# Chunks 5 to 7 of an MLP input normalised with columns on partitions, beside a long convolution

## The chip, the core and the metric

The kernel runs on one core of a Trainium2 chip. The core has five engines with an instruction stream each: TensorE (PE, matmuls; its weight loads are shown as PEld), VectorE (DVE), ScalarE (ACT), GpSimd (POOL) and SyncE (SP, which here only issues DMAs). DMAs are also issued from ACT's and POOL's streams. Engines wait for one another through semaphores; each works through its own stream in order. SBUF is the on-chip memory with 128 partitions, PSUM is the accumulator memory that PE writes. The metric is the device time of one execution in microseconds, the median of several runs.

## What is computed

```python
xn = _layernorm(x, axis=-1)              # x = A_q, 2048 rows of 448
out = x + _A_ref(xn, k, v, shift_k, ssm_k, ssm_D) + _B_ref(xn, w1, b1, w2)

# A: short causal convolution of k (4 taps), times v, then a causal convolution
#    of length 2048 per column with ssm_k (by FFT), plus kv * ssm_D; gated: xn * y
# B: h = xn @ w1 + b1 (448 -> 1792); act = h * tanh(softplus(h)); act @ w2 (1792 -> 448)
```

## The kernel before

**Two programs in one stream.** The MLP (part B) and the convolution (part A) are interleaved by hand. The 2048 rows are eight *chunks* of 256 rows (two tiles `jj` of 128 rows each), and the 1792 hidden columns are seven *pairs* of two blocks of 128. The list `pairs` has 56 entries (chunk c, pair p), entry i = 7c + p. Time is counted in *slots*, two to an entry: in the even slot 2i `mlp_slot` issues the first matmuls of entry i (`g1_mm`, line 463), in the odd slot 2i + 1 the activation (`mish`, line 479) and the second matmuls of entry i - 2 (`g2_mm`, line 493). The plans `plan` (before the MLP's part of a slot), `plan2` (after it) and `plan3` (inside `mish`, between the activations and the split) hang the convolution's steps on slots. The order of each engine's stream is the order in which this Python code runs.

**Precision.** Matmul operands are split into a high part `h` (a rounded copy in float32r, made by ACT) and a low part `l` (the difference, made by DVE): function `split`, lines 73 to 75. Three products of high and low parts are summed. Hence `XH`/`XL` for the input, `ah`/`al` (tiles `ach`, `acl`) for the activations, `w1h`/`w1l`, `w2h`/`w2l` for the weights.

**The input of a chunk.** PE contracts over partitions, so the first matmul needs the normalised input with its 448 columns on partitions (three blocks of 128; the fourth block is the last 64 columns twice, which carries high and low weights). The rows come with rows on partitions. For the next chunk c + 1, during chunk c: `ln_load` loads the rows `Q` at pair 0; `ln_stats` puts the statistics (two `bn_stats`, two `bn_aggr` on DVE, then eps on DVE and the powers on POOL) on a list `drip`, from which `dv()` draws one after other DVE work, and all that are left at p = 4 (`NP - 3`); `ln_norm` at p = 5 norms on ACT (two activations and the tail copy) into `xn`; `ln_T` (line 451) transposes each of the two row tiles by four PE matmuls with an identity (line 437), and splits the result out of PSUM (ACT line 449, DVE line 447): tile 0 in the odd slot of p = 5 ahead of `mish`, tile 1 in the even slot of p = 6 ahead of `g1_mm`.

**The convolution's middle.** In eight *octaves* o, spread over slots 63 to 90 (chunks 4 to 6): loads of `ah` and `av` from DRAM scratch (line 188, on SP), packed matmuls `h2_mm` and `v2_mm` (line 201), copies out of PSUM on ACT (`h2_out` line 212, `v2_out` line 221), six products and sums on DVE (`prod`, line 237), the inverse matmuls `i1_mm` (line 248), copies on ACT (`i1_copy`, line 256) and stores to the scratch `E` on SP (`i1_out`, line 263). `inside` puts `h2_out` and `i1_copy` into `plan3` when their slot is the odd slot of p = 5, else into `plan2`. The matmuls of a step use both PSUM buffers `pc`, so the copies of one step have to be under way before the next step's matmuls.

**The convolution's end.** From slot 94 on, four loads `e_load` from `E` (line 292, the first four on SP), a `fold` for each chunk on DVE (lines 297 and 299), the last inverse matmuls `i2_mm` (line 315; those of chunks 6 and 7 in slot 98, before the first matmul of chunk 7), and the gate on DVE and ACT. `t3` opens the last part of SBUF at its first call and then loads the constant `i2` on SP (line 275).

**The end.** The last entry (chunk 7, p = 6) does its second matmuls for each of the two row tiles, and `g2_evac` adds them to the rows `Q` that already hold input and gated convolution (line 516), and stores them. For the very last tile the addition is in two halves of 224 columns, whose stores are issued from SP (line 519) and ACT (line 520).

Of the kernel before, what the change touches and what calls it, by code (L numbers as in the profile page):

```python
# [7 lines left out]
F32 = mybir.dt.float32  # L8
F32R = mybir.dt.float32r
AF = mybir.ActivationFunctionType  # L10
ALU = mybir.AluOpType
# [3 lines left out]
S, D, F = 2048, 448, 1792  # L15
NJ = 16
NF = F // 128
NP = NF // 2
CH = 256
NCHUNK = S // CH  # L20
# [8 lines left out]
I2_AT = {98: (6, 7), 102: (0, 1), 106: (2, 3), 109: (4, 5)}  # L29
LATE = 2  # L30
MOVED = 3
WARM = (448,) * 3 + (128,)
FILL = ((64,), (128, 128))


@with_exitstack
def tile_kernel(ctx: ExitStack, tc, q, k, v, sk, hT, sD, w1, b1, w2, c_f1, c_g, c_gi, c_i2, out):
    nc = tc.nc
    V = nc.vector

    def pool(name, bufs=1, stack=ctx, **kw):
        return stack.enter_context(tc.tile_pool(name=name, bufs=bufs, **kw))

    cp = pool("consts")
    wp = pool("weights")
    mp = pool("mlp")
# [3 lines left out]
    dp = pool("scratch", space=DRAM)  # L50
# [4 lines left out]
    Dkv = dp.tile([NO * 16, 32, D], F32, name="Dkv")  # L55
    E = dp.tile([2, 2, 32, 2, NCHUNK, 2, D], F32, name="E")

    f1id = cp.tile([128, 2, 128], F32, name="f1id")
    f1, ident = f1id[:, 0], f1id[:, 1]
    mhalf = cp.tile([128, 2], F32, name="mhalf")  # L60
    b1t = cp.tile([128, NF], F32, name="b1t")
    mv = cp.tile([128, NJ, 2], F32, name="mv")
    rstd = cp.tile([128, NJ], F32, name="rstd")
    mone = cp.tile([128, 2], F32, name="mone")
    shift = cp.tile([128, NJ], F32, name="shift")


# [2 lines left out]
    w2h = wp.tile([128, NF, D], F32R, name="w2h")  # L70
    w2l = wp.tile([128, NF, D], F32R, name="w2l")

    def split(h, l, raw):
        nc.scalar.copy(h, raw)  # L74
        V.tensor_sub(l, raw, h)  # L75

    def pc():
        return pcp.tile([128, 2, 512], F32, name="pc")
# [4 lines left out]
    def dv(n=1):  # L83
        for _ in range(n):
            if drip:
                drip.pop(0)()
# [8 lines left out]
        plan2.setdefault(int(slot), []).append((fn, args))  # L95

    def inside(slot, fn, *args):
        (plan3 if slot % 2 and slot // 2 % NP == NP - 2 else plan2).setdefault(int(slot), []).append((fn, args))


    ph1 = ExitStack()
    sp1 = pool("ph1", stack=ph1)
    skb = sp1.tile([128, 4, D], F32, name="skb")
    HT, KR, VT, KV, PS, ST, SD = {}, {}, {}, {}, {}, {}, []

# [162 lines left out]
    EE, QA, Q = {}, {}, {}  # L268
# [10 lines left out]
    def late(c):  # L279
        return c >= NCHUNK - LATE  # L280
# [105 lines left out]
    def ln_parts(c):  # L386
        st = mp.tile([128, 2, 6], F32, name="bst", bufs=2)
        ve = mp.tile([128, 2], F32, name="ve", bufs=2)
        xn = mp.tile([128, 2, D + 64], F32, name="xn", tag="xn", bufs=1)
        XN[c] = xn  # L390

        def stats(jj):
            V.bn_stats(st[:, jj], Q[c][:, jj])

        def aggr(jj):
            V.bn_aggr(mv[:, 2 * c + jj], st[:, jj])  # L396

        def eps(a, b):
            V.tensor_scalar(ve[:, a:b], mv[:, 2 * c + a:2 * c + b, 1], EPS, None, op0=ALU.add)

        def power(a, b):
            r, m = (t[:, 2 * c + a:2 * c + b] for t in (rstd, shift))
            if c:
                nc.gpsimd.tensor_tensor(m, mv[:, 2 * c + a:2 * c + b, 0], mone[:, a:b], op=ALU.mult)  # L404
            nc.gpsimd.tensor_tensor(r, ve[:, a:b], mhalf[:, a:b], op=ALU.pow)
            if c:
                nc.gpsimd.tensor_tensor(m, m, r, op=ALU.mult)

        def norm(jj):
            j = 2 * c + jj  # L410
            if c:
                nc.scalar.activation(xn[:, jj, :D], Q[c][:, jj], AF.Identity, bias=shift[:, j:j + 1],
                                     scale=rstd[:, j:j + 1])
            else:
                V.tensor_scalar(xn[:, jj, :D], Q[c][:, jj], mv[:, j, 0:1], rstd[:, j:j + 1],
                                op0=ALU.subtract, op1=ALU.mult)

        def tail(a, b):
            (nc.scalar.copy if c else V.tensor_copy)(xn[:, a:b, D:], xn[:, a:b, D - 64:D])

        return stats, aggr, eps, power, norm, tail

    def ln_stats(c):
        stats, aggr, eps, power, norm, tail = ln_parts(c)
        drip.extend([lambda: stats(0), lambda: stats(1), lambda: aggr(0), lambda: aggr(1),
                     lambda: [eps(0, 2), power(0, 2)]])
        NORM[c] = norm, tail

    def ln_norm(c):
        norm, tail = NORM.pop(c)  # L430
        norm(0)
        norm(1)
        tail(0, 2)

    def transposes(c, jj, p, k0=0, k1=4):
        for kt in range(k0, k1):
# [2 lines left out]
    def x_tiles(c):  # L439
        XS[c] = (mp.tile([128, 4, CH], F32R, name="XH", tag="XH", bufs=2),  # L440
                 mp.tile([128, 4, CH], F32R, name="XL", tag="XL", bufs=2))
# [9 lines left out]
    def ln_T(c, jj):  # L451
        if jj == 0:
            x_tiles(c)
        p = g1p.tile([128, 2, CH], F32, name="pg1").rearrange("p a b -> p (a b)")
        transposes(c, jj, p)
        for lo in range(2):
            x_split(c, jj, p, lo)
# [21 lines left out]
    def mish(i, s):  # L479
        p = pairs[i][1]  # L480
        ps = P1.pop(i)
        a = mp.tile([128, 2, CH], F32, name="a", bufs=2)
        for n in range(2):
            nc.scalar.activation(a[:, n], ps[:, n], AF.Mish, bias=b1t[:, 2 * p + n:2 * p + n + 1])  # L484
        for fn, args in plan3.pop(s, ()):
            fn(*args)
        ah = mp.tile([128, 2, CH], F32R, name="ach", bufs=3)
        al = mp.tile([128, 2, CH], F32R, name="acl", bufs=3)
        split(ah, al, a)
        dv()  # L490
        AHL[i] = ah, al

    def g2_mm(i, jjs=(0, 1)):
        c, p = pairs[i]
        ah, al = AHL[i]
        for n in range(2):
            f = 2 * p + n
            for jj in jjs:
                if f == 0:
                    P2[c, jj] = g2p.tile([128, 512], F32, name="pg2")  # L500
                ps = P2[c, jj][:, :D]
                cs = slice(128 * jj, 128 * jj + 128)
                nc.tensor.matmul(ps, ah[:, n, cs], w2h[:, f], start=f == 0, stop=False)  # L503
                nc.tensor.matmul(ps, ah[:, n, cs], w2l[:, f], start=False, stop=False)  # L504
                nc.tensor.matmul(ps, al[:, n, cs], w2h[:, f], start=False, stop=f == NF - 1)  # L505

    def g2_evac(c, jjs=(0, 1)):
        x = Q[c]
        for jj in jjs:
            last = (c, jj) == (NCHUNK - 1, 1)  # L510
            if moved(c):
                nc.scalar.copy(x[:, jj], P2.pop((c, jj))[:, :D])
            else:
                p = P2.pop((c, jj))
                for cs in ((slice(0, D // 2), slice(D // 2, D)) if last else (slice(0, D),)):
                    V.tensor_add(x[:, jj, cs], p[:, cs], x[:, jj, cs])  # L516
                    dv()
            if late(c) and last:
                nc.sync.dma_start(out[:, 2 * c + jj, :D // 2], x[:, jj, :D // 2])
                nc.scalar.dma_start(out[:, 2 * c + jj, D // 2:], x[:, jj, D // 2:])  # L520
            elif late(c):
                nc.sync.dma_start(out[:, 2 * c + jj], x[:, jj])
        if not late(c):
            nc.sync.dma_start(out[:, 2 * c:2 * c + 2], x)

    def mlp_slot(s):
        i, half = divmod(s, 2)
        n = len(pairs)
        j = i - G2_LAG
        if half == 0:  # L530
            if i < n:
                c, p = pairs[i]
                if c + 1 < NCHUNK:
                    if p == (0 if c else 1):
                        ln_load(c + 1)
                    if p == (2 if c else 3):
                        ln_stats(c + 1)
                    if c == 0 or p == NP - 3:
                        dv(len(drip))
                    if p == NP - 2:  # L540
                        ln_norm(c + 1)
                    if p == NP - 1:
                        ln_T(c + 1, 1)
                g1_mm(i)
        else:
            if i < n:
                c, p = pairs[i]
                if p == NP - 2 and c + 1 < NCHUNK:
                    ln_T(c + 1, 0)
                mish(i, s)  # L550
            if 0 <= j < n - 1:
                g2_mm(j)
            elif j == n - 1:
                for jj in range(2):
                    g2_mm(j, (jj,))
                    g2_evac(pairs[j][0], (jj,))


    ctx.enter_context(tc.manual_schedule())
# [69 lines left out]

    V.memset(mhalf, -0.5)  # L630
    V.memset(mone, -1.0)
    one = cp.tile([128, NJ], F32, name="one")
    V.memset(one, 1.0)
    ve0 = cp.tile([128, 2], F32, name="ve0")
    warm = pc()

# [115 lines left out]
```

## Time and profile before

| | us |
|---|---|
| median of 3 runs | 367.59 (367.14 to 368.11) |
| the profiled execution | 368.03 |
| its span in the profile | 366.3 |

The page of the profile gives the busy time of each engine; a busy PE is not PE at its peak, since matmuls are pipelined. The chain of work that ended last is followed back from the last instruction, at each step to what released it or to the instruction before it on its engine. In lists of the chain a line has start, length and what; in lists of the timeline start, length, engine, line, operation, output and input, count, and in brackets the idle time before it with its releaser. Groups of instructions end with busy time, mean duration in ns, and the idle time of the engine ahead of them. SPq, ACTq and POOLq are DMA issues on those engines' streams. All times are from the span's start.

TensorE is granted its full clock in all 40 slices of the span:

```profile
PEclk9999999999999999999999999999999999999999
```

### The profile page before, as it was taken

Reading aid. Unit: us, or ns where it says so; the run is one execution under the profiler, and the core shown is the slowest. Engines: PE = TensorE matmul, PEld = TensorE weight load, DVE = VectorE, ACT = ScalarE, POOL = GpSimd, SP = SyncE. Lnnn points to the kernel's source line nnn. Section 1 sums busy time; section 2 is a strip of 40 time slices with the busy share of each in tenths; the row PEclk is TensorE's granted clock in tenths of the full one; section 3 lists DMA queues with packets and bytes.
Section 4 is the critical chain, followed back from the end, with each engine's and each line's share of the span. In section 5 each row is a group of like instructions: output and inputs, shape, how many; then the busy total and the mean of one; then the engine's idle time right before and its main releaser. Section 6 shows DMA issues by size and latency. Waiting matters only on the chain.

```text
span 366.3 us, 7485 instructions
## 1 busy us (share of the span) xinstructions
PE 360.1 (98%) x3134; PEld 293.2 (80%) x3134; DVE 261.6 (71%) x350; ACT 180.8 (49%) x307; POOL 24.2 (7%) x41
## 2 busy tenths in 40 slices
PE   7999999999999999999999999999999999999995
PEld 2988888888888988988877666666666889889885
DVE  4898748999999997997434747555384833897741
ACT  3987553533525343533355656557565536235450
POOL 2010000300030002000010000010000010112110
PEclk9999999999999999999999999999999999999999
DMA  8799998958499409714776497787483339649964
GB/s 292 270 314 339 370 335 219 252 170 272 100 306 275 122 18 300 201 41 100 264 236 212 142 333 221 273 242 231 177 292 131 150 106 381 226 172 283 226 120 102
DMA packets 32962, 80.73 MB, mean 220 GB/s; under 512 B 2977, under 2 KB 18338, under 8 KB 32930
## 3 DMA queue, kind: packets, MB, share of 16 engines
q1 hardware_dynamic: 25986, 57.08, 44.7%
q10 hardware_dynamic: 5072, 15.39, 15.1%
q0 software_dynamic: 1872, 7.80, 9.7%
q8 instruction: 24, 0.39, 0.5%
q14 instruction: 8, 0.07, 0.1%
HBM read 51.82 MB, written 29.82 MB: 223 GB/s over the span
## 4 chain that ended last, share of the span: by engine, by line
PE 97%; DMA 1%; ACT 0%; DVE 0%; issue 0%; DVEq 0%
PE pg L476 40%; PE pg L503 13%; PE pg L505 12%; PE pg L504 12%; PE pc L201 7%; PE pc L128 4%; PE pc L248 4%; PE pg L437 2%; PE pc L315 2%; DMA x<-in_hT_dram 1%; PE pg L639 0%; ACT L644 0%; DVE qt L516 0%; DVEq L747 0%
## 5 line engine op out<-in xcount | busy, mean ns | idle before, releaser
L484 ACT ACTIVATE a<-pg,b1t 128x256 f32<-128x256 f32 x112 | 47.1, 472 | 97.5 <-PE pg L476 79.6
L476 PE MATMUL pg<-XH,w1h 128*128 128x256 f32 x448 | 91.0, 285 | 0.2
L503 PE MATMUL pg<-w2h,ach 128*128 128x448 f32 x224 | 83.4, 372 | 0.0
L476 PEld LDWEIGHTS pg<-XH,w1h 128*128 128x128 f32 x448 | 69.7, 188 | 16.6 <-issue 13.6
L505 PE MATMUL pg<-w2h,acl 128*128 128x448 f32 x224 | 81.3, 363 | 0.0
L504 PE MATMUL pg<-w2l,ach 128*128 128x448 f32 x224 | 81.2, 362 | 0.0
L75 DVE TENSOR_TENSOR acl<-a,ach 128x512 fp32r<-128x512 f32 x56 | 38.5, 687 | 55.2 <-ACT ach L74 55.2
L476 PE MATMUL pg<-XL,w1h 128*128 128x256 f32 x448 | 69.7, 277 | 0.0
L476 PEld LDWEIGHTS pg<-XL,w1h 128*128 128x128 f32 x448 | 59.5, 188 | 0.0
L476 PE MATMUL pg<-XH,w1l 128*128 128x256 f32 x336 | 56.9, 278 | 0.0
L503 PEld LDWEIGHTS pg<-w2h,ach 128*128 128x128 f32 x224 | 42.0, 187 | 13.7 <-issue 10.1
L476 PEld LDWEIGHTS pg<-XH,w1l 128*128 128x128 f32 x336 | 47.0, 188 | 0.0
L505 PEld LDWEIGHTS pg<-w2h,acl 128*128 128x128 f32 x224 | 42.1, 188 | 2.7
L504 PEld LDWEIGHTS pg<-w2l,ach 128*128 128x128 f32 x224 | 42.1, 188 | 2.3
L74 ACT CAST ach<-a 128x512 fp32r<-128x512 f32 x56 | 34.8, 622 | 1.7
L165 DVE TENSOR_TENSOR x<-x 128x896 f32<-128x896 f32 x24 | 26.2, 1091 | 0.7
L449 ACT CAST XH<-pg 128x512 fp32r<-128x512 f32 (+1 forms) x17 | 9.5, 563 | 25.8 <-PE pg L437 25.7
L447 DVE TENSOR_TENSOR XL<-pg,XH 128x512 fp32r<-128x512 f32 (+1 forms) x17 | 10.9, 653 | 14.9 <-ACT XH L449 14.9
L134 ACT COPY st<-pc 128x896 f32<-128x896 f32 x16 | 14.5, 907 | 14.3 <-PE pc L128 6.0
L135 DVE TENSOR_TENSOR st<-pc,st 128x896 f32<-128x896 f32 x16 | 17.4, 1087 | 5.3 <-ACT st L134 5.0
L404 POOL TENSOR_TENSOR shift<-mv,mone 128x2 f32<-128x2 f32 x7 | 2.0, 287 | 276.5 <-DVE mv L396 276.5
L256 ACT COPY qe<-pc 128x896 f32<-128x896 f32 x16 | 13.8, 914 | 11.8 <-PE pc L248 11.6
(69 smaller groups left out, 390.6 us busy)
## 6 DMA issues: line engine op xcount, KB each, us to landing
Dh<-st ACTq DMA_DIRECT2D x16, 448.0 KB, 5.6
ah<-Dh SPq DMA_DIRECT2D x8, 896.0 KB, 6.3
av<-Dkv SPq DMA_DIRECT2D x8, 896.0 KB, 5.5
E<-qe SPq DMA_DIRECT2D x16, 448.0 KB, 3.7
Dkv<-st ACTq DMA_DIRECT2D x14, 448.0 KB, 6.0
kr<-in_k_dram SPq DMA_DIRECT2D x10, 448.0 KB, 7.6
x<-in_v_dram SPq DMA_DIRECT2D x8, 448.0 KB, 6.1
e<-E SPq DMA_DIRECT2D x4, 896.0 KB, 8.2
```

The costliest lines, as they stand in the source:

```text
L74: nc.scalar.copy(h, raw)
L75: V.tensor_sub(l, raw, h)
L128: nc.tensor.matmul(ps[h][64 * jj:64 * jj + 64, b, :D], f1[rg:rg + 32, 0:64], x[rg:rg + 32, jj], start=True, stop=True, tile_position=(rg, ...
L135: V.tensor_add(st[:, 0], e, st[:, 1])
L165: V.tensor_add(KV[g], KV[g], o)
L201: nc.tensor.matmul(p[32 * t:32 * t + 32, r, :D], g[rs, t, c], a[rs, t], start=True, stop=True, tile_position=(64 * r, 32 * t))
L248: nc.tensor.matmul(ps[t // 2][64 * r:64 * r + 64, t % 2, :D], gi[ts, r, c], Y[o][c][ts, r], start=c == 0, stop=c == 1, tile_position=(32 * ...
L476: nc.tensor.matmul(ps[:, n], l, r, start=n_ == 0, stop=n_ == len(mm) - 1)
L484: nc.scalar.activation(a[:, n], ps[:, n], AF.Mish, bias=b1t[:, 2 * p + n:2 * p + n + 1])
L503: nc.tensor.matmul(ps, ah[:, n, cs], w2h[:, f], start=f == 0, stop=False)
L504: nc.tensor.matmul(ps, ah[:, n, cs], w2l[:, f], start=False, stop=False)
L505: nc.tensor.matmul(ps, al[:, n, cs], w2h[:, f], start=False, stop=f == NF - 1)
```

## The change

For chunks 5, 6 and 7 (`TURNED`) the rows are brought a second time, already turned: the host lays out `qx`, in which the columns stand on partitions (four blocks, the fourth the doubled last 64) and the 256 rows of a chunk along the free dimension. `x_load` loads it on SP into the buffer that `xn` had: for chunk 5 in slot 64 (p = 4 of chunk 4), for the others at p = 2 of the chunk before.

The rows' means and scales are still computed with rows on partitions. They are put side by side into `t4` (128 x 32, four columns used), DVE transposes its 32 x 32 blocks (`ms_store`), four small DMAs store the rows to the DRAM scratch `MS`, and one DMA (`ms_load`) loads means and scales back, the same 2 x 256 numbers to every partition. `x_norm` subtracts and multiplies on DVE over 128 x 1024, and `x_cast` splits the result in one go. There are no transposes, no norm on ACT and no tail for these chunks. For chunks 5 and 6 the small DMAs are on POOL's stream, store and load behind `mish` at p = 3, and the norm at p = 5; for chunk 7 they are on SP's, the store ahead of `mish` at p = 3, load and norm behind `mish` at p = 4. The rest of `drip` is drawn at p = 3 instead of 4. The split stands in the even slot of p = 6 in all three.

`h2_out` and `i1_copy` of slots 67 and 81 (the odd slots of p = 5 in chunks 4 and 5) move out of `mish`, behind it. The tile `f1id` moves from the constants to the first phase's memory. For the very last row tile, the sum over the first twelve blocks is added to `Q` while the last pair's matmuls run, and those of the last pair are done in two ranges of columns, 256 and 192, each followed by its addition and store (`g2_end`).

```diff
+TURNED = (5, 6, 7)
...
     def inside(slot, fn, *args):
-        (plan3 if slot % 2 and slot // 2 % NP == NP - 2 else plan2).setdefault(int(slot), []).append((fn, args))
+        c, p = divmod(slot // 2, NP)
+        (plan3 if slot % 2 and p == NP - 2 and not turned(c + 1) else plan2).setdefault(int(slot), []).append((fn, args))
...
-            if c:
+            if c and not turned(c):
                 nc.gpsimd.tensor_tensor(m, m, r, op=ALU.mult)
+            if turned(c):
+                nc.gpsimd.tensor_tensor(t4[:, a:b], mv[:, 2 * c + a:2 * c + b, 0], one[:, a:b], op=ALU.mult)
+                nc.gpsimd.tensor_tensor(t4[:, 2 + a:2 + b], ve[:, a:b], mhalf[:, a:b], op=ALU.pow)
...
+    def x_load(c):
+        XN[c] = mp.tile([128, 4, CH], F32, name="xt", tag="xn", bufs=1)
+        nc.sync.dma_start(XN[c], qx[:, TURNED.index(c)])
...
+    def ms_store(c):
+        t, eng = (t3, nc.sync) if c == NCHUNK - 1 else (t2, nc.gpsimd)
+        tT = t([128, 32], "tT", 1)
+        V.transpose(tT, t4)
+        for b in range(4):
+            eng.dma_start(MS[c, :, :, b].rearrange("i j r -> (i j) r"), tT[32 * b:32 * b + 4])
+
+    def ms_load(c):
+        t, eng = (t3, nc.sync) if c == NCHUNK - 1 else (t2, nc.gpsimd)
+        BC[c] = t([128, 2, CH], "bc", 1)
+        eng.dma_start(BC[c], MS[c].rearrange("i j b r -> i (j b r)").partition_broadcast(128))
+
+    def x_norm(c):
+        for i, op in enumerate((V.tensor_sub, V.tensor_mul)):
+            op(XN[c], XN[c], BC[c][:, i:i + 1].to_broadcast([128, 4, CH]))
+
+    def x_cast(c):
+        x_tiles(c)
+        split(*XS[c], XN[c])
...
+    CUT = 256
+
+    def g2_end(i):
+        ah, al = AHL[i]
+        x = Q[NCHUNK - 1][:, 1]
+        for cols, eng in ((slice(0, CUT), nc.sync), (slice(CUT, D), nc.scalar)):
+            ps = pc()[:, 0, :cols.stop - cols.start]
+            for n in range(2):
+                f = NF - 2 + n
+                for k, (l, r) in enumerate(((ah, w2h), (ah, w2l), (al, w2h))):
+                    nc.tensor.matmul(ps, l[:, n, 128:256], r[:, f, cols], start=n + k == 0, stop=n + k == 3)
+            V.tensor_add(x[:, cols], ps, x[:, cols])
+            eng.dma_start(out[:, NJ - 1, cols], x[:, cols])
...
-                    if c == 0 or p == NP - 3:
+                    if c == 0 or p == (NP - 4 if turned(c + 1) else NP - 3):
                         dv(len(drip))
-                    if p == NP - 2:
+                    if turned(c + 1):
+                        if p == (4 if c + 1 == TURNED[0] else 2):
+                            x_load(c + 1)
+                        if p == NP - 1:
+                            x_cast(c + 1)
+                    elif p == NP - 2:
                         ln_norm(c + 1)
-                    if p == NP - 1:
+                    elif p == NP - 1:
                         ln_T(c + 1, 1)
...
-                if p == NP - 2 and c + 1 < NCHUNK:
+                t = turned(c + 1) and c + 1 < NCHUNK
+                if p == NP - 2 and c + 1 < NCHUNK and not turned(c + 1):
                     ln_T(c + 1, 0)
+                end = c + 1 == NCHUNK - 1
+                if t and p == NP - 4 and end:
+                    ms_store(c + 1)
                 mish(i, s)
+                if t and p == NP - 4 and not end:
+                    ms_store(c + 1)
+                    ms_load(c + 1)
+                if t and p == NP - 3 and end:
+                    ms_load(c + 1)
+                if t and p == (NP - 3 if end else NP - 2):
+                    x_norm(c + 1)
...
             elif j == n - 1:
-                for jj in range(2):
-                    g2_mm(j, (jj,))
-                    g2_evac(pairs[j][0], (jj,))
+                x = Q[NCHUNK - 1][:, 1]
+                V.tensor_add(x, P2.pop((NCHUNK - 1, 1))[:, :D], x)
+                g2_mm(j, (0,))
+                g2_evac(pairs[j][0], (0,))
+                g2_end(j)
```

More of the change, by code (lines that the diff above doesn't have):

```diff
@@ L36, in tile_kernel @@
 @with_exitstack
-def tile_kernel(ctx: ExitStack, tc, q, k, v, sk, hT, sD, w1, b1, w2, c_f1, c_g, c_gi, c_i2, out):
+def tile_kernel(ctx: ExitStack, tc, q, qx, k, v, sk, hT, sD, w1, b1, w2, c_f1, c_g, c_gi, c_i2, out):
     nc = tc.nc
@@ L56, in tile_kernel @@
     E = dp.tile([2, 2, 32, 2, NCHUNK, 2, D], F32, name="E")
-    f1id = cp.tile([128, 2, 128], F32, name="f1id")
-    f1, ident = f1id[:, 0], f1id[:, 1]
+    MS = dp.tile([NCHUNK, 2, 2, 4, 32], F32, name="MS")
+    t4 = cp.tile([128, 32], F32, name="t4")
     mhalf = cp.tile([128, 2], F32, name="mhalf")
@@ L64, in tile_kernel @@
     mone = cp.tile([128, 2], F32, name="mone")
+    one = cp.tile([128, NJ], F32, name="one")
     shift = cp.tile([128, NJ], F32, name="shift")
@@ L75, in split, with turned @@
         V.tensor_sub(l, raw, h)
+    def turned(c):
+        return c in TURNED
     def pc():
@@ L97, in inside @@
     def inside(slot, fn, *args):
-        (plan3 if slot % 2 and slot // 2 % NP == NP - 2 else plan2).setdefault(int(slot), []).append((fn, args))
+        c, p = divmod(slot // 2, NP)
+        (plan3 if slot % 2 and p == NP - 2 and not turned(c + 1) else plan2).setdefault(int(slot), []).append((fn, args))
     ph1 = ExitStack()
     sp1 = pool("ph1", stack=ph1)
+    f1id = sp1.tile([128, 2, 128], F32, name="f1id")
+    f1, ident = f1id[:, 0], f1id[:, 1]
     skb = sp1.tile([128, 4, D], F32, name="skb")
@@ L388, in ln_parts @@
         ve = mp.tile([128, 2], F32, name="ve", bufs=2)
-        xn = mp.tile([128, 2, D + 64], F32, name="xn", tag="xn", bufs=1)
-        XN[c] = xn
+        if not turned(c):
+            XN[c] = xn = mp.tile([128, 2, D + 64], F32, name="xn", tag="xn", bufs=1)
         def stats(jj):
@@ L402, in power @@
             r, m = (t[:, 2 * c + a:2 * c + b] for t in (rstd, shift))
-            if c:
+            if c and not turned(c):
                 nc.gpsimd.tensor_tensor(m, mv[:, 2 * c + a:2 * c + b, 0], mone[:, a:b], op=ALU.mult)
             nc.gpsimd.tensor_tensor(r, ve[:, a:b], mhalf[:, a:b], op=ALU.pow)
-            if c:
+            if c and not turned(c):
                 nc.gpsimd.tensor_tensor(m, m, r, op=ALU.mult)
+            if turned(c):
+                nc.gpsimd.tensor_tensor(t4[:, a:b], mv[:, 2 * c + a:2 * c + b, 0], one[:, a:b], op=ALU.mult)
+                nc.gpsimd.tensor_tensor(t4[:, 2 + a:2 + b], ve[:, a:b], mhalf[:, a:b], op=ALU.pow)
         def norm(jj):
@@ L433, in ln_norm @@
         tail(0, 2)
+    BC = {}
+    def ms_store(c):
[14 more added lines that the diff above has]
+        split(*XS[c], XN[c])
     def transposes(c, jj, p, k0=0, k1=4):
@@ L504, in g2_mm @@
                 nc.tensor.matmul(ps, ah[:, n, cs], w2l[:, f], start=False, stop=False)
-                nc.tensor.matmul(ps, al[:, n, cs], w2h[:, f], start=False, stop=f == NF - 1)
+                nc.tensor.matmul(ps, al[:, n, cs], w2h[:, f], start=False,
+                                 stop=f == (NF - 3 if (c, jj) == (NCHUNK - 1, 1) else NF - 1))
+    CUT = 256
[10 more added lines that the diff above has]
+            eng.dma_start(out[:, NJ - 1, cols], x[:, cols])
     def g2_evac(c, jjs=(0, 1)):
@@ L509, in g2_evac @@
         for jj in jjs:
-            last = (c, jj) == (NCHUNK - 1, 1)
             if moved(c):
@@ L513, in g2_evac @@
             else:
[L514 to L521, printed above, removed]
+                V.tensor_add(x[:, jj], P2.pop((c, jj))[:, :D], x[:, jj])
+                dv()
+            if late(c):
                 nc.sync.dma_start(out[:, 2 * c + jj], x[:, jj])
@@ L631, in tile_kernel @@
     V.memset(mone, -1.0)
-    one = cp.tile([128, NJ], F32, name="one")
     V.memset(one, 1.0)
+    V.memset(t4, 0.0)
     ve0 = cp.tile([128, 2], F32, name="ve0")
@@ L734 @@
     kpad = np.pad(a["A_k"][0], ((4, 0), (0, 0)))
+    qx = lay(a["A_q"][0])[:, :, np.r_[0:D, D - 64:D]].reshape(128, NCHUNK, 2, 4, 128)[:, list(TURNED)]
     arrs = dict(
-        q=lay(a["A_q"][0]), k=np.concatenate([lay(kpad[:S])[:, :, :][:, :4], lay(a["A_k"][0])], axis=1),
+        q=lay(a["A_q"][0]), qx=qx.transpose(4, 1, 3, 2, 0).reshape(128, len(TURNED), 4, CH), k=np.concatenate([lay(kpad[:S])[:, :, :][:, :4], lay(a["A_k"][0])], axis=1),
         v=lay(a["A_v"][0]), sk=a["A_shift_k"].T, hT=lay(a["A_ssm_k"].T), sD=a["A_ssm_D"][None],
```

## The prediction

> **What bounds the kernel now.** I read the page first, then the chain of work that ended last in order of time, then the groups by form, the timeline around the places that the diff touches, and the DMA issues.
>
> ```profile
> span 366.3 us, 7485 instructions
> PE 360.1 (98%) x3134; PEld 293.2 (80%) x3134; DVE 261.6 (71%) x350; ACT 180.8 (49%) x307; POOL 24.2 (7%) x41
> PE 97%; DMA 1%; ACT 0%; DVE 0%; issue 0%; DVEq 0%
> ```
>
> The third line is the chain: 97% of the span is TensorE following itself. So a microsecond of matmul taken out of the PE stream is a microsecond of time, unless another engine is then late; and added DVE, ACT or DMA work is free as long as no PE instruction waits for it. The profiled execution took 368.03 us, its span 366.3, the rest lies around it; the median of the runs is 367.59, so I subtract 0.44 at the end.
>
> **The transposes.** The pieces of the chain (start, length, what) around the transposes (L437) of chunks 5, 6 and 7, with neighbours that have none:
>
> ```profile
> 197.31 0.58 PE pg L437 x4
> 197.89 0.21 PE pg L503
> ...
> 201.97 0.59 PE pg L437 x4
> 202.56 2.59 PE pg L476 x22
> ...
> 211.12 2.71 PE pg L476 x22
> ...
> 215.49 0.40 PE pg L503
> ...
> 258.82 0.59 PE pg L437 x4
> 259.41 0.20 PE pg L503
> ...
> 263.48 0.59 PE pg L437 x4
> 264.07 2.51 PE pg L476 x22
> ...
> 304.81 2.51 PE pg L476 x22
> 307.32 0.44 PE pg L437 x4
> ...
> 310.17 0.44 PE pg L437 x4
> 310.61 2.59 PE pg L476 x22
> 313.20 0.21 PE pg L503
> ...
> 315.61 1.66 PE pc L315 x32
> ...
> 362.15 0.21 PE pg L505
> ```
>
> A group of four costs 0.44 between two full-width groups and 0.58 to 0.59 after the packed convolution matmuls. But the first matmul after the packed ones pays that step in any case: L503 is 0.40 there (215.49) and 0.21 behind a transpose, L476 is 2.71 there (211.12) and 2.51 to 2.59 behind one. So taking the transposes out gives: chunk 5, 0.58 + 0.21 - 0.40 = 0.39 and 0.59 + 2.59 - 2.71 = 0.47, together 0.86; chunk 6, 0.59 + 0.20 - 0.40 = 0.39 and 0.59 + 2.51 - 2.71 = 0.39, together 0.78; chunk 7, 0.44 + 0.21 - 0.21 = 0.44 and 0.44 + 2.59 - 2.51 = 0.52, together 0.96. **Sum 2.60 us.** Check: 24 transposes at 0.44/4 = 0.11 are 2.64.
>
> **What takes their place.**
>
> ```profile
> L75 DVE TENSOR_TENSOR acl<-a,ach 128x512 fp32r<-128x512 f32 x56 | 38.5, 687 | 55.2 <-ACT ach L74 55.2
> L165 DVE TENSOR_TENSOR x<-x 128x896 f32<-128x896 f32 x24 | 26.2, 1091 | 0.7
> L516 DVE TENSOR_TENSOR qt<-pg,qt 128x448 f32<-128x448 f32 x9 | 5.2, 616 | 3.8 <-PE pg L505 3.8
> L516 DVE TENSOR_TENSOR qt<-pg,qt 128x224 f32<-128x224 f32 x2 | 0.7, 386 | 0.6 <-PE pg L505 0.6
> L355 ACT CAST w1h<-kr 128x1024 fp32r<-128x1024 f32 x6 | 6.3, 1049 | 0.5 <-DMA kr<-in_w_dram 0.3
> L405 POOL TENSOR_TENSOR rstd<-ve,mhalf 128x2 f32<-128x2 f32 x7 | 6.9, 986 | 3.9 <-DVE ve L399 3.3
> L292 POOL DMA_DIRECT2D e<-E x4 | 3.0, 755 | 25.9 <-PE pc L315 25.8
> ```
>
> Per chunk DVE gets two operations of 128x1024: from 512 wide at 0.69 and 896 at 1.09 the slope is 1.05 ns a column, so 1.23 us each, 2.45 together; one 1.23 us subtract replaces two of 512. ACT loses the norm, its tail and two casts, and gets one cast of 1.05. POOL gets one more pow, about 1 us. Nothing of this is on PE, and it is free if the next PE reader still finds its data:
>
> ```profile
> 269.14 1.08 DVE L237 TENSOR_TENSOR yc<-yc,yd 128x896 f32<-128x896 f32 x1
> ...
> 270.79 1.01 PE L248 MATMUL pc<-ya,gi 32*64 32x448 f32 x16
> ...
> 296.57 1.85 SPq L263 DMA_DIRECT2D E<-qe  x2
> 298.48 0.60 SPq L275 DMA_DIRECT2D i<-in_c_i_dram  x1
> ...
> 309.81 0.69 DVE L75 TENSOR_TENSOR acl<-a,ach 128x512 fp32r<-128x512 f32 x1 [0.70 <-ACT ach L74]
> 310.42 1.09 DVE L297 TENSOR_TENSOR ex<-e 128x896 f32<-128x896 f32 x1
> ...
> 312.55 1.08 DVE L297 TENSOR_TENSOR ex<-e 128x896 f32<-128x896 f32 x1
> ...
> 363.11 0.36 ACTq L520 DMA_DIRECT2D out_dram<-qt  x1
> ```
>
> *Chunks 5 and 6, among the octaves.* The tightest place is chunk 6: the last product ends at 270.22 and PE wants it at 270.79, 0.57 us of slack. Before, DVE stood there behind casts that ACT made after the transposes. After, the last activation pair of chunk 5 no longer waits for them: I follow DVE through the split, 2.45 of norm, four products, the 1.23 subtract and two products, and it ends near 268.3 where PE, 1.64 earlier, comes at 269.2: slack 0.9, no stall. In chunk 5 the same walk leaves 1.7. The turned means have two pairs of some 8.6 us (202.56 to 211.12): four stores and a load at 0.76 us each on POOL's queue, and two landings of at most 4.3 (below), are 12.4 of 17. The h2 and inverse copies that move out of the mish (slots 67 and 81) come behind one 0.62 cast and gain the wait for the transposes. Cost: 0. If this cover were gone, each microsecond of late products would be one of PE.
>
> *Chunk 7, on SP.* Here is the new wait.
>
> ```profile
> e<-E SPq DMA_DIRECT2D x4, 896.0 KB, 8.2
> E<-qe SPq DMA_DIRECT2D x16, 448.0 KB, 3.7
> g<-in_c_g_dram SPq DMA_DIRECT2D x8, 128.0 KB, 4.3
> skb<-in_sk_dram SPq DMA_DIRECT2D x1, 896.0 KB, 9.9
> out_dram<-qt SPq DMA_DIRECT2D x1, 112.0 KB, 1.7
> ```
>
> (size, median us to landing.) SP ends the E stores at 298.42 and the i2 load at 299.08; PE's lead of 1.64 makes that 297.44. By then t4 is there, since the statistics are drawn one pair sooner. Four stores at 0.36 to 0.60 of issue, 1.7 to 3.7 to land, the load's issue, and 1.7 to 4.3 to land: the broadcast arrives between 302.7 and 308.4; I take 304.6, nearest the small rows, as nothing else is in the queues then. Behind the norm on DVE stand, in order, a split (0.61 of pitch), two folds (2.13 each, from 310.42 to 312.55) and the second half of the split of chunk 7's input. PE wants the second fold half way through L315, 316.44 - 2.60 = 313.84. So the limit for the arrival is 313.84 - 2.45 - 0.61 - 4.26 = **306.5**; two microseconds to spare, and up to 1.9 of stall at the slow end. On SP itself the four e loads are held behind the broadcast load, issued near 302.2 instead of 299.5: the second lands within 8.2, near 310.9, and its fold may start at 311.7. Also held, narrowly.
>
> The Trainium skill ("DMA: Bandwidth & Descriptors", Anatomy of one DMA) gives a DMA a fixed cost of about 2.0 us; by it the arrival would be an estimated 304. The 1.7 us row agrees roughly, the 3.7 and 4.3 rows are of larger transfers.
>
> The three copies of q are 512 KB each on SP, behind av's load, so they delay no load that PE is near to; cost 0 to a few tenths, taken as 0.
>
> **The end.** PE's last twelve matmuls of 448 take 0.20 each (362.15). After: six of 448, 1.20; six of 256 at 2.51/22 = 0.114, 0.68; six of 192, which no row has: between 0.114 x 192/256 = 0.086 and 0.114, so 0.52 to 0.68, I take 0.60. PE ends 0.08 later (0 to 0.16). Behind it before: two adds, then the last issue at 363.11, 0.75 after PE's end at 362.36. After: one add of 192, 386 - 32 x 1.03 = 353 ns, and the issue, 0.41 after. The add of the partial sum lies beside twelve matmuls' time. **Gain 0.34 - 0.08 = 0.26**, 0.18 to 0.34.
>
> A rule speaks against narrow matmuls: the Trainium skill ("TensorE: Matmul & The Clock Gate", LDWEIGHTS) has a weight load take columns/1.2 ns, 107 ns for 128 columns, which would keep six matmuls of 192 at 0.64 and the gain at 0.22. No row here is narrow enough to settle it.
>
> **Sum.** 2.60 + 0.26 = 2.86; 368.03 - 2.86 = 365.17, less 0.44: **364.7 us**.
>
> **Rivals.**
> - *Chunk 7's statistics come late* (arrival past 306.5): a stall at L315 of 0 to 1.9, so 364.7 to 366.6. For it: two DMA round trips in series on one in-order queue. Against: an idle chip's DMA. 0.20.
> - *The narrow end costs more*: if 192 and 256 columns ran at the packed f32 pace (1.66/32 x 8 = 0.415 for 448), 192 would take 0.18, PE ends 0.48 + 0.08 later: 365.2. 0.08.
> - *Nothing gained*: PE's place is taken by ACT or DVE in the octaves, where each pair has three evacuations; the 2.6 us become waits and the time stays at 367.3 to 367.6. Against: chain 97% PE and ACT 49% busy. 0.12.
> - *Slower*: the broadcast of one row to 128 partitions is slow by its form. The one such row, skb, took 9.9 us. With that landing the arrival is 302 + 0.4 + 9.9 = 312.3, the stall 5.8, the time 370.5. It decides against the change from an arrival of 306.5 + 2.9 = 309.4 on. Against: skb moved 3.5 times the bytes while all weights were loading. 0.08.
> - My forecast: 0.52.
>
> **Numbers.** About 0.3% (1.1 us) is what a measurement of this kernel can tell from no change. Faster: forecast, late statistics and narrow end, 0.80; within: 0.12; slower: 0.08. The range is 363.9 (a few short waits of PE on ACT go too) to 366.6 (the slow end of the late statistics); it leaves out the last two rivals.
>
> **What would show it.** No L437 in chunks 5 to 7 and PE's chain still near 97%; PE's start of chunk 7's first L476 2.6 earlier; SP's broadcast load landing before 306.5 and DVE's folds without a wait ahead of them; the last matmuls at 0.09 to 0.11 and the last issue 0.4 after PE's end. Wrong would be a PE wait on DVE at L315 or L248, or an idle DVE ahead of the new norm that ends on a DMA and is followed by an idle PE.

## The result and the profile after

The changed kernel takes 364.95 us in the median of 8 runs (364.41 to 367.31), the kernel before 367.62 beside it (8 runs, 366.77 to 368.78). The ratio is 0.9939 with a 95% interval of 0.9918 to 0.9960. 364.7 was forecast. Two of the six runs of experiment 5, at 401.59 and 848.23 us, fell in a slow state and are left out of its figures.

| | before | after |
|---|---|---|
| profiled execution, us | 368.03 | 364.76 |
| its span | 366.3 | 363.0 |

The head of the page of the changed kernel and its chain by engine:

```profile
span 363.0 us, 7477 instructions
PE 357.9 (99%) x3116; PEld 291.1 (80%) x3116; DVE 269.5 (74%) x358; ACT 175.8 (48%) x295; POOL 31.7 (9%) x51
...
PE 99%; DVE 0%; issue 0%
```

DVE got 8 us more work and ACT lost 5, and the chain is still PE following itself. To place the gain, two marks of the chain of the kernel before: the last forward transform of the convolution, which ends before anything is turned, and the last octave's inverse matmuls.

```profile
173.43 0.94 PE pc L128 x16
...
293.10 1.69 PE pc L248 x32
```

The same marks in the chain of the changed kernel (L137, L257), with the places where transposes stood, the last inverse matmuls (L324) and the end:

```profile
172.65 0.94 PE pc L137 x16
...
200.80 2.71 PE pg L514 x22
...
261.46 2.72 PE pg L514 x22
...
290.70 1.69 PE pc L257 x32
...
307.31 2.51 PE pg L514 x22
312.23 1.67 PE pc L324 x32
...
357.77 1.36 PE pc L556 x12
359.16 0.36 DVE qt L557
```

Between the marks lie 119.67 us before and 118.05 after: chunks 5 and 6 gave **1.62**. From the second mark to L324 (315.61 before) it is 22.51 and 21.53: chunk 7 gave **0.98**. The experiments below repeat both numbers: with all three chunks turned the two stretches were 118.05 to 118.15 and 21.52 or 21.53 in six more profiles (`x1`, `x3`, `x5`, `x9`, `x10`, `x11`); with nothing turned (`x8`) they were 119.75 and 22.51. No transposes (L437 before, L475 in the changed kernel) are left there, and the first wide matmuls behind the packed ones cost 2.71 and 2.72, as they did wherever no transpose took the step for them. The rest of the 3.3 us between the two profiles is not the change's: 0.78 was there ahead of the first mark, and 0.73 of it is there at the first transform, which waited for the very first load and began at 6.82 before, and began at 6.09 after.

### The profile page after: what moved, and what is told of

Read it like the earlier page. It is cut to its first block, busy times and chain, and to the rows that moved or that the text cites. A ratio compares the mean times of both kernels' runs of the same rounds, so it can differ in the third digit from the quotient of the medians.

```text
span 363.0 us, 7477 instructions
## 1 busy us (share of the span) xinstructions
PE 357.9 (99%) x3116; PEld 291.1 (80%) x3116; DVE 269.5 (74%) x358; ACT 175.8 (48%) x295; POOL 31.7 (9%) x51
## 4 chain that ended last, share of the span: by engine, by line
PE 99%; DVE 0%; issue 0%
PE pg L514 40%; PE pg L541 13%; PE pg L543 12%; PE pg L542 12%; PE pc L210 7%; PE pc L137 4%; PE pc L257 4%; PE pc L324 2%; PE pc L704 1%; PE pg L475 1%; PE pc L556 0%; PE pg L704 0%; DVE qt L557 0%; DVE mhalf L695 0%; DVE t L698 0%
## 5 line engine op out<-in xcount | busy, mean ns | idle before, releaser
L414 POOL TENSOR_TENSOR rstd<-ve,mhalf 128x2 f32<-128x2 f32 (+1 forms) x9 | 9.0, 1000 | 132.4 <-DVE ve L408 132.2
L144 DVE TENSOR_TENSOR st<-pc,st 128x896 f32<-128x896 f32 x16 | 17.4, 1086 | 4.2 <-ACT st L143 3.9
L165 DVE TENSOR_TENSOR x<-kr,skb 128x896 f32<-128x896 f32 x16 | 17.3, 1084 | 2.0 <-DMA kr<-in_k_dram 2.0
L145 DVE TENSOR_TENSOR st<-pc,st 128x896 f32<-128x896 f32 x16 | 17.5, 1092 | 0.6
```

The costliest lines, as they stand in the source:

```text
L144: V.tensor_add(st[:, 0], e, st[:, 1])
L145: V.tensor_sub(st[:, 1], e, st[:, 1])
L165: V.tensor_mul(o, KR[g - u // 2], skb[:, u:u + 1].to_broadcast([128, 2, D]))
```

## The experiments

All but one (7) change a single thing in the changed kernel, with what belongs to it; the code is shown in part, and `...` marks what is left out. The theory was: the transposes taken out of PE's stream are the gain; the means' round trips are hidden, chunk 7's with little to spare.

**1. The old end put back** (`x1_old_end`): the last entry's code, `g2_evac` with it, is that of the kernel before.

```diff
...
-                g2_mm(j, (0,))
-                g2_evac(pairs[j][0], (0,))
-                g2_end(j)
+                for jj in range(2):
+                    g2_mm(j, (jj,))
+                    g2_evac(pairs[j][0], (jj,))
```

> The change with the old end: the last row tile is added in two halves of 224 after undivided matmuls. Theory (the transposes out of the PE stream are nearly all of the gain): 2.6 us under the kernel before, 365.0 to 365.2; from the start of the last six matmuls to the last issue 2.12 us again, as before, against 1.94 in the changed kernel. Rival (the end by columns is a large part): 1 us or more of the gain gone, 366 or above.

Measured 364.70 (6 runs, 364.20 to 365.30), beside a kernel before of 367.89: ratio 0.9910 (0.9891 to 0.9928). Nothing of the gain is lost without the new end; the time is a little under its forecast.

**2. Only the end by columns** (`x8_end_only`), the complement: nothing is turned, the input `qx` is gone and `f1id` is among the constants again.

```diff
-TURNED = (5, 6, 7)
+TURNED = ()
...
```

> Nothing turned: the kernel before with the end by columns alone. Theory: all of the gain but 0.2 goes, 367.3 to 367.9, the same as before within the measurement; 1.94 us from the last six matmuls to the last issue, and about 3.4 behind it. Rival (the end matters): 0.5 us or more under the kernel before.

Measured 367.71 (12 runs) against 368.30: ratio 0.9987 (0.9974 to 1.0000), so the new end is worth between nothing and 1.0 us. These medians lie 0.59 apart, and by themselves they don't exclude the rival's 0.5. Its profile and experiment 1 speak against it: from the start of the last matmuls to the span's end it took 5.29 us, the kernel before 5.31 (table in 8), and without the new end nothing was lost. The stretches between the marks are as long as before the change (above), so the transposes are the gain.

**3. Chunk 7 transposed again** (`x2_turn56`), with its identity loaded into the last part of SBUF:

```diff
-TURNED = (5, 6, 7)
+TURNED = (5, 6)
...
```

> Only chunks 5 and 6 turned; chunk 7 is transposed on PE as before (its identity is loaded again in the last phase); the new end stays. Theory: chunk 7's eight transposes come back, 0.96 us, so 365.9 to 366.1; in the chain L315's first piece after chunk 6 comes 1.64 earlier than before, not 2.6, counted from the same start of the convolution. Rival (the round trip for chunk 7's means costs what its transposes cost): within 0.3 us of the changed kernel, 364.7 to 365.2. If late arrivals of chunk 7's means make the changed kernel's slower runs (366.4 to 367.3 beside 364.4 to 365.0), the runs of this kernel lie within 1 us of each other.

Measured 366.42 (7 runs, 365.12 to 367.18), 0.3 above the forecast's upper end; its fastest is 1.0 above the fastest of the next kernel on the same chip. In its profile L327, the last inverse matmuls, comes 22.51 us behind the second mark, exactly as before the change, so chunk 7's 0.98 is back. But the runs do not lie within 1 us, and the profiled one, 367.18, the slowest, shows one cause. A part of its chain among the octaves of chunk 4:

```profile
193.25 6.47 DMA bc<-MS
...
199.74 1.24 DVE xt L470
...
202.26 1.05 ACT XH L77
203.31 0.81 ACT vs L230
...
204.17 2.54 PE pc L257 x32
```

This is chunk *5*'s round trip, not chunk 7's: the broadcast load lands at 199.72, DVE norms, ACT casts the input's high part, and only then makes the copies `vs` that stand behind that cast in its stream. PE's inverse matmuls wait for those copies (the PSUM buffers), and take 2.54 instead of 1.69 with 0.34 of wait ahead. That is 1.2 us. Another 0.6 is lost before anything is turned: a forward transform at 100.62 takes 1.54 for 0.94. What held it up was not traced.

**4. No wait for chunk 7's means** (`x3_no_wait7`): chunk 7 is normed with chunk 6's means and scales, which stand in DRAM long before.

```diff
-        eng.dma_start(BC[c], MS[c].rearrange("i j b r -> i (j b r)").partition_broadcast(128))
+        eng.dma_start(BC[c], MS[min(c, 6)].rearrange("i j b r -> i (j b r)").partition_broadcast(128))
```

> Chunk 7 is normed with chunk 6's means and scales, so its broadcast load doesn't wait for chunk 7's four stores (which are still made). Theory: the load is issued some 1.6 us sooner and DVE's wait ahead of the norm, 2.82 us in the changed kernel, shrinks to about 1.2; PE didn't wait for it, so the median stays at 364.6 to 365.1. Rival (PE does wait for the round trip somewhere, or in some runs): the median or the slower runs come down by 0.5 us or more.

Measured 364.78 (6 runs, 364.12 to 366.00). DVE's wait ahead of the norm went altogether (the forecast left 1.2), the median stayed: PE does not pay for chunk 7's round trip. Two runs at 365.95 and 366.00 remain, so slower runs come without chunk 7's wait too.

**5. Chunk 7's load and norm one pair later** (`x4_late7`, once more as `x4b_late7` for its profile): the prediction's slower case, brought about.

```diff
-                if t and p == NP - 3 and end:
+                if t and p == NP - 2 and end:
                     ms_load(c + 1)
-                if t and p == (NP - 3 if end else NP - 2):
+                if t and p == NP - 2:
```

> Chunk 7's broadcast load and norm one pair later (p = 5, as for chunks 5 and 6), so that on SP the load stands behind the four e loads. Theory: the means arrive behind 3.6 MB, about 6 us later than now, where the changed kernel has 0.6 us to spare: PE waits at the second fold's matmul or the input split for 4 to 6 us, 369 to 371, slower than the kernel before. Rival (the norm's place doesn't matter, as DVE is 74% busy): 364.7 to 365.5.

> The kernel with chunk 7's load and norm one pair later once more, for its profile. Theory: the broadcast load stands behind the e loads on SP and lands near 311; DVE idles for it until then, and PE waits on DVE ahead of L324 in slot 98 for about 5 us; 370.3 to 370.7. Rival (the time is lost elsewhere, such as the e loads themselves): DVE's idle time ahead of the norm is under 3 us.

Measured 370.33 to 370.69 in four runs (median 370.55), ratio 1.0062 (1.0042 to 1.0082): slower than the kernel before. The run of the profile took 370.29. First the changed kernel's own timeline at this place (start, length, engine, line and what; in brackets DVE's idle time and its releaser):

```profile
299.96 0.34 SPq L463 DMA_DIRECT2D bc<-MS  x1
...
305.08 2.48 DVE L467 TENSOR_TENSOR xt<-xt,bc 128x1024 f32<-128x1024 f32 x2 [2.82 <-DMA bc<-MS]
...
311.33 1.09 DVE L308 TENSOR_TENSOR e<-e 128x896 f32<-128x896 f32 x1
```

DVE waits 2.82 for the means, and the second fold ends at 312.42; PE wants it half way through L324, near 313.06. So 0.6 us are to spare. One pair later the load stands behind the e loads (timeline, then chain of `x4b_late7`):

```profile
311.59 2.48 DVE L467 TENSOR_TENSOR xt<-xt,bc 128x1024 f32<-128x1024 f32 x2 [4.43 <-DMA bc<-MS]
...
317.24 1.09 DVE L308 TENSOR_TENSOR e<-e 128x896 f32<-128x896 f32 x1
```

```profile
312.22 2.96 issue
315.18 4.23 PE pc L324 x32
```

The means come 6.5 us later, and PE loses 2.96 ahead of L324 (the chain names no releaser; DVE's first sum of the folds ends at 315.07, just ahead of PE's start) and 2.56 in it (4.23 for 1.67), together 5.5. The second fold ends at 318.33, 5.9 later than in the changed kernel; less the 0.6 to spare that is 5.3, so PE pays nearly one for one. The other 0.2 fits the clock: behind PE's wait of 2.96 the granted clock was 0.60 of full speed from 315.2 to 319.4, where the changed kernel had 1.00 for the same matmuls.

**6. The changed kernel again, and with earlier stores** (`x0_after_again`, `x9_early_store`). After the third experiment the suspicion was on chunk 5. In the changed kernel's timeline, its stores, its broadcast load and its norm:

```profile
183.88 2.11 POOL L458 DMA_DIRECT2D MS<-tT  x4 [2.67 <-DVE tT L456]
...
192.49 0.58 POOL L463 DMA_DIRECT2D bc<-MS  x1 [6.50 <-issue]
...
197.66 2.48 DVE L467 TENSOR_TENSOR xt<-xt,bc 128x1024 f32<-128x1024 f32 x2 [0.55 <-DMA bc<-MS]
```

POOL stands idle 2.67 for DVE's turning, which sits behind the activation's split; then 6.5, for which the profile names no releaser; the load reads what the stores write, and their row is 5.6 in the median from issue to landing. Then the load takes 5.2. DVE already waits 0.55 in this run of 364.76, which PE still doesn't feel. The other profiles with late stores show where it begins: DVE waited 0.50 to 0.84 in `x1`, `x3`, `x4b` and `x11`, and the inverse matmuls took their 1.69; 1.22 in `x5`, and they took 1.78; 2.12 and 2.32 in `x0` (below) and `x2`, and PE lost 1.0 and 1.2. The edit turns ahead of the split:

```diff
-                if t and p == NP - 4 and end:
+                if t and p == NP - 4:
                     ms_store(c + 1)
                 mish(i, s)
                 if t and p == NP - 4 and not end:
-                    ms_store(c + 1)
                     ms_load(c + 1)
```

> The changed kernel as it is, beside the next three on one chip. 364.4 to 367.3 as so far, with two groups of times: about 364.2 to 365.0, and some at 365.9 and above.

> As the changed kernel, but the turning and the four stores of the means of chunks 5 and 6 stand ahead of the activation's split on DVE, not behind it. Theory (the changed kernel's slower runs are those in which chunk 5's means, sent over POOL's queue, come after about 199; DVE waited 0.5 to 0.8 us for them in three profiles and 2.3 in the one of 367.18): POOL's stores start near 181.5 instead of 183.9, the means land near 195 and DVE's norm of chunk 5 has no wait on a DMA ahead of it; the group of times at 365.9 and above goes, the median is 364.2 to 364.9 and all runs lie within 1.2 us. Rival (the slower runs come from the start or another place common to all kernels): spread and median as in the changed kernel.

The changed kernel took 365.12 (7 runs, 364.52 to 369.40; ratio 0.9923, 0.9901 to 0.9945), with early stores 365.06 (6 runs, 364.59 to 365.75). The timeline of the latter:

```profile
181.98 2.11 POOL L458 DMA_DIRECT2D MS<-tT  x4 [0.55 <-DVE tT L456]
...
190.26 0.58 POOL L463 DMA_DIRECT2D bc<-MS  x1 [6.17 <-DMA ah<-Dh]
...
197.25 2.48 DVE L467 TENSOR_TENSOR xt<-xt,bc 128x1024 f32<-128x1024 f32 x2
```

DVE's wait is gone, as expected, here and in the next experiment's profile; the median is not lower and misses the forecast's 364.9, as in most profiles PE had lost nothing. Whether the runs are steadier is not shown. Of the kernels with late stores that turn all three chunks (experiment 5 apart), 7 of 29 runs are at 365.9 or above; of the two with early stores (this and the next), none of 12, which drawn at random would come about 7 times in 100. But the line at 365.9 was taken from the earlier runs, and with a line at 365.5 it is 7 of 29 and 3 of 12. And chunk 5 isn't the only cause. The profiled run of `x0_after_again`, 369.40, had the first of these pieces at the head of its chain; the second is the same piece in `x1_old_end` (start, length, what):

```profile
1.34 6.94 DMA x<-in_hT_dram
```

```profile
1.34 4.27 DMA x<-in_hT_dram
```

The first load landed 2.7 us later, which shifts the whole kernel; its second mark is 4.61 behind that of the run of 364.76. Of these, its first transform begins 2.32 later, 1.30 more are lost before the first mark, and 1.00 is chunk 5's wait, with the same four links as above. The 1.30 is TensorE's clock. PE stood idle for 2.51 us until that load had landed, and the clock granted to it was then 0.73 (8.4 to 9.7), 0.50 (to 11.1) and 0.64 (to 12.9) of full speed, and 1.00 again from 13. The first four transposes in this run's chain, then in that of the run of 364.76, where the clock was 1.00:

```profile
9.73 1.05 PE pg L475 x4
```

```profile
7.15 0.59 PE pg L475 x4
```

From the first transform to the first wide matmuls it is 4.57 us here and 3.14 there. In `x1_old_end` PE waited 0.70 for the load and in the kernel before 1.09, and the clock stayed at 1.00.

**7. Early stores and the old end** (`x10_early_old_end`), both edits above together.

> The early stores and the old end (undivided last matmuls, two additions of 224). If the end by columns is worth its 0.18 us from the last six matmuls to the last issue, this is 0.2 slower than with the early stores alone; if the span's rest behind the last issue (2.84 and 3.19 us with the old end, 3.37 to 3.48 with the new) takes that back, it is 0 to 0.3 faster. A difference of 0.2 is at the edge of what five rounds can tell; the two stretches in the profile tell it apart: 2.12 and about 3.0 here.

364.83 (6 runs, 364.04 to 365.71), ratio 0.9913 (0.9893 to 0.9934). Against 365.06 and 365.12 this is no difference that the runs can tell.

**8. Narrower last matmuls** (`x5_cut320`, `x11_cut224`): `CUT = 320` and `CUT = 224`, one run each, for the profile: 364.71 and 364.43.

> The end by columns cut at 320 instead of 256, so the last six matmuls have 128 columns. If a matmul's pace is its columns (0.0446 us per 100 columns x 100, from 2.51/22 for 256), they take 0.057 each and the twelve 0.86 + 0.34 = 1.20 us; if it can't go below the 0.106 that 192 columns took (0.65 for six, as by the 107 ns of a 128-column weight load), 0.86 + 0.64 = 1.50.

> The end by columns cut at 224, so that the two stores are of the same size as with the old end. If the sizes of the stores (256 and 192 columns) make the 0.4 us longer stretch behind the last issue, it is 2.8 to 3.2 again; if the closer order of the three last stores does, it stays at 3.3 to 3.5.

(In the first text, 2.51/22 for 256 columns is 0.0446 us per 100 columns.) Of six matmuls of 128 columns in the timeline of `x5_cut320`, the first three:

```profile
358.57 0.22 PE L556 MATMUL pc<-w2h,ach 128*128 128x128 f32 x1
358.63 0.27 PE L556 MATMUL pc<-w2l,ach 128*128 128x128 f32 x1
358.74 0.27 PE L556 MATMUL pc<-w2h,acl 128*128 128x128 f32 x1
```

After the first, they start 0.11 apart, and so do those of 192 and 224: the twelve took 1.51 as the second alternative had it. From 224 columns down to 128 a matmul gets no shorter here. For the stores, the stretch behind the last issue came out at 3.25 with the cut at 224, between the two answers: not settled.

What all ends show, worked out from the first start of the last row tile's six or twelve matmuls, the last issue and the span:

| end | matmuls' start to last issue | last issue to the span's end |
|---|---|---|
| old: before, x1, x10 | 2.12, 2.12, 2.12 | 3.19, 2.84, 2.85 |
| 256 and 192: after, x0, x8, x9 | 1.94 each | 3.45, 3.44, 3.35, 3.33 |
| 320 and 128: x5 | 2.02 | 3.19 |
| 224 and 224: x11 | 1.96 | 3.25 |

The 0.18 that the new end wins ahead of the last issue does not reach the span's end: the two stretches together are 5.31, 4.96 and 4.97 with the old end, 5.27 to 5.39 with the new one and 5.21 with the other two cuts. Behind the last issue SP waits for the last stores, here in the changed kernel and then in `x10_early_old_end` (total, times, longest; the kernel before has 1.3 in 3 times):

```profile
SPq L813 <- DMA out_dram<-qt: 1.9, 3, 1.2
```

```profile
SPq L802 <- DMA out_dram<-qt: 1.0, 2, 0.6
```

Counted from the matmuls' start, SP is done with its own last issue after 1.70 with the new end and after 2.16 with the old; it comes to the wait 0.46 sooner and stands in it 0.9 longer than in `x10_early_old_end`, 0.6 longer than in the kernel before. Whether the sizes of the stores or their closer order costs it is open.

## Why the prediction was right

- *Transposes.* Forecast 1.64 for chunks 5 and 6 and 0.96 for chunk 7, measured 1.62 and 0.98. Experiment 3, which gives chunk 7's back, and 2, in which nothing is turned, agree. The point that made the number was to charge the step behind the packed matmuls to those, not to the transposes.
- *The DVE norm at no cost.* The two operations took 2.48 as forecast, and chunk 6's octaves show no PE wait. Held.
- *Chunk 7's round trip.* The mechanism was right, the sizes less: the broadcast took 5.1 us to land, not 3, and the arrival at 305.08 is, on the old start's clock, 305.86 of the 306.5 allowed. 0.6 us to spare, where the text said two. It took the load for alone in the queues; the four e loads were issued 0.4 us behind it (300.39). In experiment 4, where it was issued 1.5 sooner, at 298.42, the means were there by 302.05, with the e loads just as close behind; what made the 5.1 is open. And it called the rows of 3.7 and 4.3 larger transfers, but the row of 1.7 is 112 KB and that of 4.3 is 128 KB, so size does not tell them apart. Experiment 5 shows the price beyond the spare time, and that the slower rival's stall was a real possibility, though by the load's place and not by its form: 370.55 with load and norm one pair later.
- *Chunk 5's round trip* is the step that was wrong without showing in the median. The text let it fit with 12.4 of 17 us. The window is shorter, 183.9 to 197.1, because the turning stands behind the split; the two landings took 6.5 and 5.2, where the text allowed 4.3 at most although 8.2 stood in the same list; and the walk followed DVE's stream alone. That the median did not show it is luck: 0.55 of wait was too little for PE. The wait passes to ACT, where the input's cast stands ahead of the copies that PE needs.
- *The end.* Mis-sized: 0.26 forecast, 0.18 measured up to the last issue, as six matmuls of 192 took 0.11 each, the upper bound, and those of 256 took 0.118; and nothing after the stores' landing, which the sum had left as it was. What was overlooked cost 0.3 us of the sum and lies within the measurement. (The narrow end's rival was priced too low: at the packed pace the six matmuls of 256 would cost 0.74 more, which its 365.2 leaves out. Neither width ran at that pace.) The Trainium skill ("TensorE: Matmul & The Clock Gate", LDWEIGHTS) gives a 128-column weight load 107 ns, which the text set against narrow matmuls; the trace agrees with it, 0.11 for 128, 192 and 224 columns, but does not show that the weight load sets this pace.
- *A landing's price.* The broadcast load took 5.1 us, and from POOL's last store to its load it was 6.5. The Trainium skill's fixed cost of about 2.0 us ("DMA: Bandwidth & Descriptors", Anatomy of one DMA), which that section gives for DMAs on GpSimd's path and the text applied to SP's, made an estimated arrival of 304; the rows here are far above it.

## What to carry to other kernels

Where one engine carries 97% of the chain, price a removal by the difference of two neighbourhoods of that engine, with and without the operation, not by the operation's own length. Where a value now travels through DRAM, count the window from the instruction that really starts it, follow the wait onto every engine whose stream it enters, and move the start forward as far as it goes: that was free here and took DVE's wait away in both profiles, though steadier runs are not shown. A wait of TensorE can cost more than its own length: behind 2.5 us of idle at the start, a lower clock cost 1.3 more. An end that issues its last DMA sooner has not ended sooner until that DMA has landed.

## What was not expected of the hardware

Small transfers were slow to land: four stores of 512 bytes each on POOL's queue were followed by the load that needs them only 6.2 to 6.9 us after the last issue (6.50 in the changed kernel, 6.17 in `x9`, 6.94 in `x2`), among the convolution's loads. A float32r matmul with its own 128-column weight load did not go below 0.11 us from 256 columns down to 128 (0.114 to 0.118 at 256, 0.147 at 320). And the landing of the first load moves a whole run: 4.3 us in one profile, 6.9 in another. Behind a TensorE idle for 2.5 us in `x0_after_again` and 3.0 in `x4b_late7` the granted clock was 0.50 to 0.73 and 0.60 for some 4 us.
